# One queue for all cache loads, and a new order of the last tiles, in a batched attention decode step

## The chip, the cores and the metric

The kernel runs on one core of a Trainium2 chip. Its metric is the time of one execution on the device, in microseconds (us). Runs of this kernel lie within 2 us of each other, so a change of about 0.2% can be told from none.

The core has five engines that run side by side, each with its own instruction stream: TensorE (PE in the profile), VectorE (DVE), ScalarE (ACT), GpSimd (POOL) and SyncE (SP). Data comes from memory into the on-chip buffer by DMA. Sixteen DMA engines do the moving; a transfer is issued by an engine's instruction and goes through that engine's queue. SP's queue is q1 in the profile, ScalarE's is q10.

## What is computed

Two independent attention blocks, A and B, each with one new token for 8 sequences, 32 heads of size 128, and a cache of 4096 keys and values for each sequence and head:

```python
q = (x @ wq).reshape(B, Sq, H, Dh).transpose(0, 2, 1, 3)
scores = einsum("bhqd,bhkd->bhqk", q, k_cache) * (Dh ** -0.5)
p = softmax(scores, axis=-1)
o = einsum("bhqk,bhkd->bhqd", p, v_cache)
y = o.transpose(0, 2, 1, 3).reshape(B, Sq, H * Dh) @ wo
...
return concatenate([a, b], axis=-1)
```

Here B = 8, Sq = 1, D = 1024, H = 32, Sk = 4096, Dh = 128, all in bfloat16. The caches are 2 x 2 x 268 MB, and each element of them is used once.

## The kernel before, in words

**Tiles.** The work is cut into 128 units (NQ), each one sequence and four heads (HQ = 4). Unit n belongs to block `blk = n // 8` (four heads, all 8 sequences), and there are 16 blocks, 8 of A and then 8 of B. A unit has one K tile and one V tile of 4 MB, 128 partitions by 32 KB: 32 partitions to a head, and in each partition 128 consecutive cache rows of 128 numbers. A unit's K tile is worked in four chunks (NR = 4), so there are 512 steps (NS), and step s is chunk r of unit n with `n, r = divmod(s, 4)`.

**One step.** VectorE multiplies the chunk by the query in place (line 262), then adds the upper half of each row to the lower (L267, "fold"). TensorE adds up groups of 16 with an identity matrix (L275, "eacc"), and VectorE reduces what is left to 32 scores per partition (L281, "red"). After the fourth chunk VectorE takes the maximum (L287, L291), and ScalarE computes the exponentials, one instruction to a head (L297, L304), into the tile `PM`, a ring of two units.

**PV and after.** The products with V are 32 matmuls per unit on TensorE (L317, "PV"), in four parts, in a bank `pv_ps[n % 2]`. ScalarE copies the bank (L323), TensorE extracts the useful part of it (L331, "ext"). After the eighth unit of a block follow the sums of the exponentials (L338), the division (L345, L346) and the product with the block's rows of WO (L357, "proj"). After the last block of A and of B the result goes out (L362, L363, and two DMAs).

**Order.** There is no scheduler: the Python loop over `s` in the last part of `_build_kernel` adds each operation to its engine's list, and the engine runs its list in that order. An operation waits on semaphores for the operations that it depends on, and holds up what is behind it on the same engine. `make_pv` for unit v is called seven steps (PL = 7) after its first score step, two parts in step 4v + 7 and two in 4v + 8; ext, norm and proj follow 2, 3 and 4 steps after the first. The PVs so stand between the score matmuls of later units; the PVs of units 125 and 126 are called in steps 507 to 512, that of 127 in 515 and 516, after the last score step (511).

**Loads.** `order` is the sequence in which tiles take slots in a ring of five (NSLOT): K0, then K(n+1) and V(n) in turn. Tile i uses slot i % 5 and waits until tile i - 5 is done with: a K tile by its fourth eacc, a V tile by its last PV. `load_tiles`, called at the end of each step, issues the next tiles for which that operation has been put in the list. K tiles are issued from SP and V tiles from ScalarE. The last V tile is loaded in four pieces of 1 MB, each with its own semaphore. SP also issues x at the start, WQ (2 MB, 8 times, in packets of 2 KB) and WO (1 MB, 16 times, in packets of 2 KB), each when the one before it has been used.

Of the kernel before, what the change touches and what calls it, by code (L numbers as in the profile page):

```python
# [4 lines left out]
ACTF = mybir.ActivationFunctionType  # L5
ALU = mybir.AluOpType
AX = mybir.AxisListType
BF16 = mybir.dt.bfloat16
# [17 lines left out]
def _at(ops, key, none=None):  # L26

    first = key[0] if isinstance(key, tuple) else key
    return none if first < 0 else ops[key]


class _Program:
# [9 lines left out]
    def add(self, eng, emit, deps=(), dma_key=None):  # L42
        op = _Op(eng, emit, list(deps), dma_key)
        if dma_key is not None:
            self.counts[dma_key] = self.counts.get(dma_key, 0) + 16
            op.token = (dma_key, self.counts[dma_key])
        for d in op.deps:
            if not (d.eng == "pe" and eng == "pe"):
                d.sig = True
        self.ops[eng].append(op)  # L50
        return op
# [31 lines left out]
def _build_kernel(nc, caches, out):  # L83
    B, Sq, D = caches[0][0].shape
# [5 lines left out]
    HQ = 4  # L90
    MP = 128 // HQ
    T = Sk // MP
    CT = 32
    NR = T // CT
# [3 lines left out]
    NB = NC * H // HQ  # L98
    NQ = NB * B
    NS = NQ * NR  # L100
    NSLOT = 5
    PL = 7
# [3 lines left out]
    with es:  # L106
        block = es.enter_context(nc.Block())
        sb = lambda name, shape, dt: es.enter_context(nc.sbuf_tensor(name, shape, dt))
# [13 lines left out]
        s_sb = sb("s_sb", [128, 3, T], FP32)  # L122
        rmax = sb("rmax", [128, 2], FP32)
        ngm = sb("ngm", [128, 2], FP32)
        bias = sb("bias", [128, 2], FP32)
        rsum = sb("rsum", [128, 2, B], FP32)
        PM = sb("PM", [128, 2, T, HQ], BF16)
        accS = sb("accS", [128, 2, 512], BF16)
        rl = sb("rl", [128, 2, HQ * B], FP32)
        on_sb = sb("on_sb", [128, 2, HQ, B], BF16)  # L130
# [14 lines left out]
        P = _Program()  # L145
        add = P.add

        def dma(out_ap, in_ap, key, deps, eng="sp"):
            return add(eng, lambda e: e.dma_start(out_ap, in_ap), deps, dma_key=key)


        def pool_select(view, base, pattern, dep):
# [10 lines left out]
        for j in range(HQ):  # L163
            c_mask = add("dve", lambda e, j=j: e.memset(mask[MP * j:MP * (j + 1), j:j + 1], 1.0), [c_mask])
        c_PM = add("pool", lambda e: e.memset(PM[:], 0.0))
        c_pv = [add("dve", lambda e, t=t: e.memset(t[:], 0.0)) for t in pv_ps]

        opT, opMul, opEacc, opRed, opRmax, opNgm, opBias, opExp = {}, {}, {}, {}, {}, {}, {}, {}
        opPV, opAcc, opExt, opQb, opQbc, opQ, opQs, opWQ, opWO = {}, {}, {}, {}, {}, {}, {}, {}, {}
        opLsum, opNorm, opProj = {}, {}, {}  # L170
        last = {"misc": None}
        outs = []


        order = [("k", 0)]
        for n in range(NQ):
            if n + 1 < NQ:
                order.append(("k", n + 1))
            order.append(("v", n))
        pos = {kn: i for i, kn in enumerate(order)}  # L180
        issued = [0]

        def tile_of(kind, n):
            return ring[:, pos[(kind, n)] % NSLOT, :]

        def freed(i):

            kind, n = order[i]
            return opEacc.get(NR * n + NR - 1) if kind == "k" else opPV.get((n, NR - 1))

        def load_tiles():
            while issued[0] < len(order):
                i = issued[0]
                dep = None
                if i >= NSLOT:
                    dep = freed(i - NSLOT)
                    if dep is None:
                        return
                kind, n = order[i]
                blk, b = divmod(n, B)  # L200
                c, hb = divmod(blk, H // HQ)
                from_ = caches[c][1 if kind == "k" else 2][b, hb * HQ:(hb + 1) * HQ].rearrange("u (m t) d -> (u m) (t d)", m=MP)
                to = tile_of(kind, n)
                if i == len(order) - 1:
                    for r in range(NR):
                        cols = slice(r * CT * Dh, (r + 1) * CT * Dh)
                        opT[("v", n, r)] = dma(to[:, cols], from_[:, cols], ("vl", r), [dep], "act")
                else:
                    op = dma(to, from_, ("t", i % NSLOT), [dep], "act" if kind == "v" else "sp")
                    for r in range(NR):  # L210
                        opT[(kind, n, r)] = op
                issued[0] += 1
# [28 lines left out]
        def make_qbc(n):  # L241

            blk, b = divmod(n, B)

            def emit(e):
                for j in range(HQ):
                    i = e.matmul(misc[MP * j:MP * (j + 1), 0:Dh], selb[:, b, :], q_sb[:, blk % 4, j * Dh:(j + 1) * Dh],  # L247
                                 start=True, stop=True, tile_position=(0, MP * j))
                return i
            opQb[n] = add("pe", emit, [c_selb, opQs[blk], last["misc"]])  # L250
            opQbc[n] = last["misc"] = add(
                "act", lambda e: e.activation(qbc[:, n % 2, :], misc[:, 0:Dh], ACTF.Copy),  # L252
                [opQb[n], _at(opMul, NR * (n - 2) + NR - 1)])
# [41 lines left out]
        def make_exp(n):  # L295
            blk, b = divmod(n, B)
            opBias[n] = add("act", lambda e: e.activation(bias[:, n % 2:n % 2 + 1], ngm[:, n % 2:n % 2 + 1], ACTF.Copy, scale=scale),  # L297
                            [opNgm[n]] + _at(opExp, n - 2, []))
            opExp[n] = []
            for j in range(HQ):  # L300
                rows = slice(MP * j, MP * (j + 1))

                def emit(e, j=j, rows=rows):
                    return e.activation(PM[rows, n % 2, :, j], s_sb[rows, n % 3, :], ACTF.Exp, bias=bias[rows, n % 2:n % 2 + 1],  # L304
                                        scale=scale, accum_out=rsum[rows, blk % 2, b:b + 1])
                opExp[n].append(add("act", emit, [opBias[n], _at(opPV, (n - 2, NR - 1)), _at(opLsum, blk - 2), c_PM]))


        def make_pv(n, r):
            bank = pv_ps[n % 2]  # L310
            v = tile_of("v", n)

            def emit(e):
                for g in range(r * RG // NR, (r + 1) * RG // NR):
                    for q in range(4):
                        t = 4 * (4 * g + q)
                        i = e.matmul(bank[32 * q:32 * q + 4 * HQ, :], PM[:, n % 2, t:t + 4, :].rearrange("p t j -> p (t j)"),  # L317
                                     v[:, t * Dh:(t + 4) * Dh], start=(g == 0), stop=(g == RG - 1), tile_position=(0, 32 * q))
                return i
            opPV[(n, r)] = add("pe", emit, opExp[n] + [opT[("v", n, r)], _at(opAcc, n - 2), c_pv[n % 2]])  # L320
# [61 lines left out]
        make_q(0, 0)  # L382
        make_qbc(0)

        for s in range(NS + 16):
            n, r = divmod(s, NR)
            if s < NS:
                make_mul(s)
            if 1 <= s <= NS:
                make_red(s - 1)  # L390
            if r == 0 and 1 <= n <= NQ:
                make_rmax(n - 1)
            if s < NS:
                fold = make_fold(s)
            if r == 0 and 1 <= n <= NQ:
                make_ngm(n - 1)
                make_exp(n - 1)

            for k in range(2):
                v, w = divmod(s - PL - k, NR)  # L400
                if w == 0 and 0 <= v < NQ:
                    make_pv(v, 2 * k)
                    make_pv(v, 2 * k + 1)
                    if k == 1:
                        make_acc(v)
            v, w = divmod(s - PL - 2, NR)
            if w == 0 and 0 <= v < NQ:
                make_ext(v)
            if r == 2 and n + 1 < NQ:
                make_qbc(n + 1)  # L410
            if s < NS:
                make_eacc(s, fold)
            v, w = divmod(s - PL - 3, NR)
            if w == 0 and v >= 0 and v % B == B - 1 and v < NQ:
                make_norm(v // B)
            v, w = divmod(s - PL - 4, NR)
            if w == 0 and v >= 0 and v % B == B - 1 and v < NQ:
                make_proj(v // B)
            v, w = divmod(s - PL - 8, NR)
            if w == 0 and v >= 0 and v % B == B - 1 and v // B + 1 < NB:  # L420
                load_wo(v // B + 1)
            m, w = divmod(s, 2 * B * NR)
            if m == 0 and w == 3:
                make_q(0, 1)
            if w == 7 and m + 1 < NM:
                load_wq(m + 1)
            if w in (27, 35) and m + 1 < NM:
                make_q(m + 1, 0 if w == 27 else 1)
            load_tiles()
        assert issued[0] == len(order) and len(opProj) == NB  # L430

# [59 lines left out]
```

## Time and profile before

| | |
|---|---|
| Median of three runs | 2620.51 us (2619.95 to 2621.73) |
| Span of the profiled execution | 2618.7 us |
| The same execution's time | 2620.51 us |
| VectorE busy | 2080.5 us, 79% |
| TensorE matmuls busy | 1312.7 us, 50% |
| ScalarE busy | 445.8 us, 17% |
| Data moved | 1108.58 MB, 423 GB/s over the span |
| Share of q1 and q10 in the DMA engines' time | 51.1% and 47.9% |
| VectorE waiting for a K tile ahead of L262 | 501.0 us, 60 times |
| ScalarE waiting for the maximum ahead of L297 | 1594.5 us |

The page cuts the span into 40 slices of 65.5 us. In the row DMA each digit is the busy share of the DMA engines in tenths, and GB/s is what they moved. A row of a group of instructions has the line, the engine, the operation, what it writes and reads with its shape, how often, then busy time in us and mean ns of one, and then the idle time of the engine just before them with what ended most of it. A row of DMA issues has the tile and its source, the issuing queue, how many, the size of each and the median time from issue to landing in us. A row of a stretch of time has its bounds, its length, the busy us of PE, PEld (the weight loads of TensorE), DVE, ACT and POOL with the number of instructions, the share of full clock that TensorE was granted, the DMA share and GB/s.

### The profile page before, as it was taken

What the parts mean: (1) busy time and instruction counts of PE and PEld (TensorE: products, weight loads), DVE (VectorE), ACT (ScalarE), POOL (GpSimd) and SP (SyncE); (2) the same over time, 40 slices, a digit from 0 to 9 for tenths busy, and PEclk for the clock granted to TensorE, in tenths of its full rate; (3) what the DMA queues carried; (4) which work ended last, traced back from release to release, by engine and by line L of the source; (5) the groups of instructions that cost most, each with busy time, mean ns of one, the idle gap of its engine ahead of it and who ended that gap; (6) DMA issues with size and microseconds to landing.
All of it is one profiled execution on the core that took longest, in us unless ns stands there. A gap on an engine that the chain in (4) does not pass through costs nothing.

```text
span 2618.7 us, 18877 instructions
## 1 busy us (share of the span) xinstructions
PE 1312.7 (50%) x7568; PEld 368.8 (14%) x7568; DVE 2080.5 (79%) x1833; ACT 445.8 (17%) x1427; POOL 3.2 (0%) x15
## 2 busy tenths in 40 slices
PE   2555453653536535365353554536445364453645
PEld 0111110111101111011110111101111011111111
DVE  4988795986969869698695977959779696886957
ACT  0211111221112111121121211212112111111212
POOL 0000000000000000000000000000000000000000
PEclk9666665666667667676675766756766666666766
DMA  9999999999999999999999999999999999999996
GB/s 414 426 432 429 430 431 420 432 429 427 429 427 431 428 425 429 420 431 426 429 431 427 431 430 422 430 426 431 430 422 425 431 430 428 420 432 419 432 430 261
DMA packets 54247, 1108.58 MB, mean 423 GB/s; under 512 B 4576, under 2 KB 4608, under 8 KB 21008
## 3 DMA queue, kind: packets, MB, share of 16 engines
q1 hardware_dynamic: 35296, 570.50, 51.1%
q10 hardware_dynamic: 18864, 536.88, 47.9%
q8 instruction: 59, 0.97, 0.1%
q14 instruction: 28, 0.23, 0.0%
HBM read 1107.33 MB, written 0.03 MB: 423 GB/s over the span
## 4 chain that ended last, share of the span: by engine, by line
DVE 48%; DMA 32%; another core or an unknown queue 14%; PE 4%; issue 2%; ACT 1%; SPq 0%
DVE ring L262 27%; DMA ring<-in_A_k_cache_dram 15%; DVE ring L267 14%; DMA ring<-in_B_k_cache_dram 9%; DVE s_sb L281 6%; DMA ring<-in_B_v_cache_dram 5%; DMA ring<-in_A_v_cache_dram 3%; PE red L275 2%; PE pv L317 1%; DVE rmax L287 1%; PE proj L357 0%; ACT PM L304 0%; DVE ngm L291 0%; PE o L338 0%
## 5 line engine op out<-in xcount | busy, mean ns | idle before, releaser
L262 DVE TENSOR_TENSOR ring<-ring,qbc 128x4096 bf16<-128x4096 bf16 x512 | 1165.4, 2276 | 501.0 <-DMA ring<-in_A_k_cache_dram 259.4
L275 PE MATMUL red<-ring,ident 128*128 128x512 bf16 x2048 | 820.9, 545 | 938.8 <-DVE ring L267 938.8
L267 DVE TENSOR_TENSOR ring<-ring 128x2048 bf16<-128x2048 bf16 x512 | 622.1, 1215 | 0.0
L317 PE MATMUL pv<-ring,PM 128*16 128x512 bf16 x4096 | 397.2, 505 | 63.6 <-DMA ring<-in_B_v_cache_dram 36.6
L275 PEld LDWEIGHTS red<-ring,ident 128*128 128x128 bf16 x2048 | 203.7, 121 | 1378.9 <-DVE ring L267 1124.0
L281 DVE TENSOR_REDUCE s_sb<-red 128x32 f32<-128x512 f32 x512 | 350.0, 684 | 12.4 <-PE red L275 12.4
L304 ACT ACTIVATE PM<-s_sb,bias 32x128 bf16<-32x128 f32 x512 | 295.0, 576 | 15.1
L297 ACT ACTIVATE bias<-ngm 128x1 f32<-128x1 f32 x128 | 26.0, 203 | 1594.8 <-DVE ngm L291 1594.5
L331 PE MATMUL o<-E,accS 128*128 128x4 bf16 x512 | 33.6, 170 | 271.4 <-ACT accS L323 271.4
L317 PEld LDWEIGHTS pv<-ring,PM 128*16 128x16 bf16 x4096 | 98.9, 101 | 343.0 <-issue 215.7
L304 ACT ACTIVATION_READ_ACCUMULATOR PM<-s_sb,bias 32x1 f32 x512 | 128.1, 250 | 0.0
L252 ACT ACTIVATE qbc<-misc 128x128 bf16<-128x128 f32 x128 | 35.6, 278 | 370.6 <-PE misc L247 370.6
L323 ACT ACTIVATE accS<-pv 128x512 bf16<-128x512 f32 x128 | 76.4, 597 | 5.7 <-PE pv L317 2.2
L331 PEld LDWEIGHTS o<-E,accS 128*128 128x128 bf16 x512 | 22.8, 104 | 349.6 <-ACT accS L323 349.6
L233 PE MATMUL misc<-WQ,xT 128*8 128x512 bf16 x128 | 35.7, 429 | 20.7 <-DMA WQ<-in_A_wq_dram 20.7
L287 DVE TENSOR_REDUCE rmax<-s_sb 128x1 f32<-128x128 f32 x128 | 36.6, 286 | 4.4
L238 ACT ACTIVATE q_sb<-misc 8x512 bf16<-8x512 f32 x16 | 9.4, 587 | 171.7 <-PE misc L233 171.7
L247 PE MATMUL misc<-q_sb,selb 8*32 8x128 bf16 x512 | 37.1, 281 | 0.8 <-ACT q_sb L238 0.8
L247 PEld LDWEIGHTS misc<-q_sb,selb 8*32 8x32 bf16 x512 | 13.4, 96 | 104.3 <-issue 104.3
L291 DVE TRANSPOSE_TENSOR_REDUCE ngm<-rmax 128x1 f32<-128x32 f32 x128 | 26.2, 205 | 0.0
L338 PE MATMUL o<-rsum,mask 128*128 128x8 f32 x128 | 24.6, 320 | 0.0
L338 PEld LDWEIGHTS o<-rsum,mask 128*128 128x128 f32 x128 | 23.4, 274 | 0.0
(25 smaller groups left out, 55.7 us busy)
## 6 DMA issues: line engine op xcount, KB each, us to landing
ring<-in_A_v_cache_dram ACTq DMA_DIRECT2D x64, 4096.0 KB, 27.0
ring<-in_A_k_cache_dram SPq DMA_DIRECT2D x64, 4096.0 KB, 36.0
ring<-in_B_k_cache_dram SPq DMA_DIRECT2D x64, 4096.0 KB, 34.6
ring<-in_B_v_cache_dram ACTq DMA_DIRECT2D x63, 4096.0 KB, 26.0
WQ<-in_A_wq_dram SPq DMA_DIRECT2D x4, 2048.0 KB, 46.4
WO<-in_A_wo_dram SPq DMA_DIRECT2D x8, 1024.0 KB, 54.3
WQ<-in_B_wq_dram SPq DMA_DIRECT2D x4, 2048.0 KB, 63.5
WO<-in_B_wo_dram SPq DMA_DIRECT2D x8, 1024.0 KB, 54.9
```

The source lines that it names most:

```text
L233: i = e.matmul(misc[0:B, :], xT[:, (c * DC + k) * B:(c * DC + k + 1) * B], WQ[:, k, f * HQ * Dh:(f + 1) * HQ * Dh], start=(k == 0), stop=( ...
L247: i = e.matmul(misc[MP * j:MP * (j + 1), 0:Dh], selb[:, b, :], q_sb[:, blk % 4, j * Dh:(j + 1) * Dh], start=True, stop=True, tile_position ...
L262: opMul[s] = add("dve", lambda e: e.tensor_tensor(v, v, qbc[:, n % 2, :].unsqueeze(1).to_broadcast([128, CT, Dh]), ALU.mult), [opT[("k", n ...
L267: return add("dve", lambda e: e.tensor_tensor(v[:, :, 0:64], v[:, :, 0:64], v[:, :, 64:128], ALU.add), [opMul[s]])
L275: i = e.matmul(dst, ident[:], v[:, :, j, :], start=(j == 0), stop=(j == 3))
L281: opRed[s] = add("dve", lambda e: e.tensor_reduce(s_sb[:, n % 3, r * CT:(r + 1) * CT], red_ps[s % 2][:, :].rearrange("p (t w) -> p t w", w ...
L287: opRmax[n] = add("dve", lambda e: e.tensor_reduce(rmax[:, n % 2:n % 2 + 1], s_sb[:, n % 3, :], AX.X, ALU.max), [opRed[NR * n + NR - 1]])
L304: return e.activation(PM[rows, n % 2, :, j], s_sb[rows, n % 3, :], ACTF.Exp, bias=bias[rows, n % 2:n % 2 + 1], scale=scale, accum_out=rsum ...
L317: i = e.matmul(bank[32 * q:32 * q + 4 * HQ, :], PM[:, n % 2, t:t + 4, :].rearrange("p t j -> p (t j)"), v[:, t * Dh:(t + 4) * Dh], start=( ...
L323: opAcc[n] = add("act", lambda e: e.activation(accS[:, n % 2, :], pv_ps[n % 2][:], ACTF.Copy), [opPV[(n, NR - 1)], _at(opExt, n - 2)])
L331: x = e.matmul(o_ps[blk % 2][:, HQ * b:HQ * (b + 1)], accS[:, n % 2, i * 128:(i + 1) * 128], E16[:, i, :], start=(i == 0), stop=(i == 3))
L338: x = e.matmul(o_ps[blk % 2][:, 64 + B * j:64 + B * (j + 1)], mask[:, j:j + 1].to_broadcast([128, 128]), rsum[:, blk % 2, :], start=True, ...
```

## The change

All tile loads are issued from SP. The last five tiles come in the order K126, K127, V125, V126, V127, where it was K126, V125, K127, V126, V127. The PVs of the last three units start in steps 512, 514 and 516, after the last score step, so the exponentials of three units have to be kept, and `PM` becomes a ring of three. The order of all other operations is as before.

```diff
-        PM = sb("PM", [128, 2, T, HQ], BF16)
+        PM = sb("PM", [128, 3, T, HQ], BF16)
...
-        def dma(out_ap, in_ap, key, deps, eng="sp"):
-            return add(eng, lambda e: e.dma_start(out_ap, in_ap), deps, dma_key=key)
+        def dma(out_ap, in_ap, key, deps):
+            return add("sp", lambda e: e.dma_start(out_ap, in_ap), deps, dma_key=key)
...
         order = [("k", 0)]
-        for n in range(NQ):
-            if n + 1 < NQ:
-                order.append(("k", n + 1))
-            order.append(("v", n))
+        for n in range(NQ - 3):
+            order += [("k", n + 1), ("v", n)]
+        order += [("k", NQ - 2), ("k", NQ - 1), ("v", NQ - 3), ("v", NQ - 2), ("v", NQ - 1)]
...
-                        opT[("v", n, r)] = dma(to[:, cols], from_[:, cols], ("vl", r), [dep], "act")
+                        opT[("v", n, r)] = dma(to[:, cols], from_[:, cols], ("vl", r), [dep])
                 else:
-                    op = dma(to, from_, ("t", i % NSLOT), [dep], "act" if kind == "v" else "sp")
+                    op = dma(to, from_, ("t", i % NSLOT), [dep])
...
-                    return e.activation(PM[rows, n % 2, :, j], s_sb[rows, n % 3, :], ACTF.Exp, bias=bias[rows, n % 2:n % 2 + 1],
+                    return e.activation(PM[rows, n % 3, :, j], s_sb[rows, n % 3, :], ACTF.Exp, bias=bias[rows, n % 2:n % 2 + 1],
                                         scale=scale, accum_out=rsum[rows, blk % 2, b:b + 1])
-                opExp[n].append(add("act", emit, [opBias[n], _at(opPV, (n - 2, NR - 1)), _at(opLsum, blk - 2), c_PM]))
+                opExp[n].append(add("act", emit, [opBias[n], _at(opPV, (n - 3, NR - 1)), _at(opLsum, blk - 2), c_PM]))
...
+        pv_at = {max(NR * v + PL, NS + 2 * (v - NQ + 3) if v >= NQ - 3 else 0): v for v in range(NQ)}
...
             for k in range(2):
-                v, w = divmod(s - PL - k, NR)
-                if w == 0 and 0 <= v < NQ:
+                v = pv_at.get(s - k)
+                if v is not None:
                     make_pv(v, 2 * k)
                     make_pv(v, 2 * k + 1)
                     if k == 1:
                         make_acc(v)
-            v, w = divmod(s - PL - 2, NR)
-            if w == 0 and 0 <= v < NQ:
+            v = pv_at.get(s - 2)
+            if v is not None:
                 make_ext(v)
```

The calls of `make_norm`, `make_proj` and `load_wo` are put in terms of `pv_at` in the same way, 3, 4 and 8 steps after the PV's first. PV's matmuls read `PM[:, n % 3, ...]`.

More of the change, by code (lines that the diff above doesn't have):

```diff
@@ L316, in emit @@
                         t = 4 * (4 * g + q)
-                        i = e.matmul(bank[32 * q:32 * q + 4 * HQ, :], PM[:, n % 2, t:t + 4, :].rearrange("p t j -> p (t j)"),
+                        i = e.matmul(bank[32 * q:32 * q + 4 * HQ, :], PM[:, n % 3, t:t + 4, :].rearrange("p t j -> p (t j)"),
                                      v[:, t * Dh:(t + 4) * Dh], start=(g == 0), stop=(g == RG - 1), tile_position=(0, 32 * q))
@@ L412, in _build_kernel @@
                 make_eacc(s, fold)
-            v, w = divmod(s - PL - 3, NR)
-            if w == 0 and v >= 0 and v % B == B - 1 and v < NQ:
+            v = pv_at.get(s - 3)
+            if v is not None and v % B == B - 1:
                 make_norm(v // B)
-            v, w = divmod(s - PL - 4, NR)
-            if w == 0 and v >= 0 and v % B == B - 1 and v < NQ:
+            v = pv_at.get(s - 4)
+            if v is not None and v % B == B - 1:
                 make_proj(v // B)
-            v, w = divmod(s - PL - 8, NR)
-            if w == 0 and v >= 0 and v % B == B - 1 and v // B + 1 < NB:
+            v = pv_at.get(s - 8)
+            if v is not None and v % B == B - 1 and v // B + 1 < NB:
                 load_wo(v // B + 1)
```

## The prediction

> **What bounds the kernel now.** I read the page's load rows first, then the issues with their landing times, then the DMA queues over short stretches, the stretches that follow each stall, and last the end of the timeline.
>
> ```profile
> DMA  9999999999999999999999999999999999999996
> GB/s 414 426 432 429 430 431 420 432 429 427 429 427 431 428 425 429 420 431 426 429 431 427 431 430 422 430 426 431 430 422 425 431 430 428 420 432 419 432 430 261
> L262 DVE TENSOR_TENSOR ring<-ring,qbc 128x4096 bf16<-128x4096 bf16 x512 | 1165.4, 2276 | 501.0 <-DMA ring<-in_A_k_cache_dram 259.4
> ring<-in_A_v_cache_dram ACTq DMA_DIRECT2D x64, 4096.0 KB, 27.0
> ring<-in_A_k_cache_dram SPq DMA_DIRECT2D x64, 4096.0 KB, 36.0
> WO<-in_A_wo_dram SPq DMA_DIRECT2D x8, 1024.0 KB, 54.3
> ```
>
> All 16 DMA engines are busy from start to end at about 430 GB/s, and VectorE, the busiest engine (79%), stands 501.0 us waiting for K tiles. The loads are the bound. The odd row is the last: a 1 MB weight load takes 54.3 us to land, a 4 MB V tile 27.0. The DMA view of 2360 to 2376 us, with such a WO load on the way, says why (queue: packets, MB, share of the engines):
>
> ```profile
> q10 hardware_dynamic: 196, 5.37, 78.2%
> q1 hardware_dynamic: 475, 1.47, 23.0%
> ```
>
> q1 is SP's queue, q10 ScalarE's. SP sends many 2 KB packets and ScalarE few of 32 KB, so K and WO get a quarter of the time. The K tile behind WO comes late, VectorE stands still (21.79 us before the K at 2555.07), no slot comes free, and some 40 us later both queues are nearly empty. Of ten 20 us stretches in which that happens, these are five, with a quiet stretch of 140 us for comparison; the last two columns are DMA share and GB/s:
>
> ```profile
> 120.00:260.00 140.00, 79.66 (x440) 22.38 (x432) 116.68 (x102) 24.89 (x79) 0.00 (x0) 0.64 1.00 431
> 940.00:960.00 20.00, 9.97 (x56) 2.60 (x56) 19.93 (x19) 3.40 (x11) 0.00 (x0) 0.60 0.97 406
> 1600.00:1620.00 20.00, 12.64 (x76) 3.34 (x76) 19.97 (x18) 3.39 (x11) 0.00 (x0) 0.67 0.94 396
> 1920.00:1940.00 20.00, 11.50 (x64) 3.11 (x64) 19.96 (x18) 3.67 (x12) 0.00 (x0) 0.67 0.97 405
> 2240.00:2260.00 20.00, 11.01 (x60) 2.92 (x60) 19.96 (x19) 6.02 (x21) 0.00 (x0) 0.67 0.92 385
> 2400.00:2420.00 20.00, 11.94 (x66) 3.18 (x65) 19.96 (x18) 6.21 (x20) 0.00 (x0) 0.67 0.96 401
> ```
>
> The other five (from 440, 620, 1100, 1280 and 2560 us) have 421, 417, 403, 417 and 415 GB/s. The ten average 406.6, so against 431 they lose (431 - 406.6)/431 x 200 us = 11.3 us. The other K stalls cost VectorE time but no DMA time.
>
> Then the end:
>
> ```profile
> 2585.00:2590.00 5.00, 4.29 (x38) 1.01 (x36) 5.00 (x5) 0.00 (x0) 0.00 (x0) 0.76 1.02 429
> 2590.00:2595.00 5.00, 1.04 (x4) 0.31 (x4) 4.97 (x7) 2.98 (x10) 0.00 (x0) 0.92 0.81 339
> 2595.00:2600.00 5.00, 2.42 (x9) 0.75 (x10) 5.00 (x5) 0.13 (x1) 0.00 (x0) 0.50 0.00 0
> ```
>
> The data ends near 2594; the last piece of V lands at 2595.5 (issued at 2578.55, 17.0 to landing). The span ends at 2618.7: 23.2 us in which VectorE works off K126 and K127, since K125 had come late. The median of the runs is 2620.51, 1.8 more than the span, and I add that 1.8 at the end.
>
> **The change, part by part.**
>
> *V on SP's queue.* ScalarE loses 131 issues (64 + 63 + 4) at 0.334 us. It stands 1594.5 us waiting for ngm, which hides them: 0. SP gains 131 issues at 0.33 us, 43 us spread over waits of 2142.5 us for PV: 0. The waits themselves stay (a K slot comes free by the fourth score matmul, a V slot by the last PV), but now they stand in one line. K(n+1) lands at time 0; from the trace its slot is free at +17.3 (2555.07 to 2572.40) and V(n)'s at +18.3 (2573.37). A 4.19 MB tile at 431 GB/s takes 9.75 us, so in load order V(n) lands at 9.75, K(n+2) at 19.5, V(n+1) at 29.2 and K(n+3), issued at -1.2, at 39. The next issue, V(n+2), goes out at 17.3, when 39 - 17.3 = 21.7 us of data are still queued; that work hides every wait in the line. Without it each microsecond of lateness costs a microsecond. WO and WQ now pass in their turn: 1.05 MB at the 406 GB/s of 60 to 70 us, where WQ goes alone with K, is 2.6 us instead of 54.3. V(n) is needed by PV 14.2 us after K(n+1) (2569.25) and lands at 9.75; with a WO ahead at 12.4, with a WQ at 14.9. The last makes TensorE wait 0.7 us, in VectorE's slack of 19.5 - 16.2 = 3.3 us per tile pair (16.2 from 2555.07 to 2571.23): 0.
>
> What goes, then, is the running dry. Its bounds are 0 (the line stalls as often) and 20 (every byte at 431: 1108.58/431 ms = 2572, plus a first byte at 1.8, against 2594). The second can't be reached, since the 2 KB packets run at 406. I take the 11.3 that is seen in the ten stretches: **-11.3**.
>
> Here a rule of the Trainium skill speaks against the change. "DMA: Bandwidth & Descriptors", in Rules for kernel authors and in Issuing engines are not separate DMA queues, says that all issuing engines feed the same 16 DMA engines, and that spreading loads over them saves only issue time. Taken alone that makes this part worth nothing and the sum 11.3 us higher. The 78.2% against 23.0% above disagree for a stream with unequal packets: there the split decides which tile comes first.
>
> *The start.* The first large load was V0 from ScalarE at 0.74 us; now it is WQ at 1.49, behind x. The engines idle 0.75 us longer; at worst 1.5, if the slow first 20 us repeat, at best 0. I take **+0.8**. K0 lands near 20 us instead of 38, which helps only VectorE: 0.
>
> *The last five tiles.* K126, K127, V125, V126, V127. Let T be the landing of the last piece: 2595.5 - 11.3 + 0.8 = 2585.0. K126 lands four tiles before, T - 39.0. VectorE has finished K125 by then (it lands at T - 58.5, takes 16.2). From the first multiplication of K126 to the last exp the trace has 2571.23 to 2609.04 = 37.8 us, so exps(127) end at T - 1.2: the work that stood behind the stream is now beside it.
>
> *The last PVs.* PV125 and the first half of PV126 run after the last score matmul (2605.08 in the trace, 4.0 before the last exp, hence T - 5.2), 32 matmuls in 1.9 us, 16 in 0.95: done by T - 2.3. Then TensorE waits for the copy of bank 125, which stands behind exp(127) in ScalarE: 0.85 us from copy to next matmul (2609.06 to 2609.89 now), T - 0.35. Half of PV126 to T + 0.6; first half of PV127 to 1.55; extraction of 126 0.25; second half of PV127 to 2.75. From there the old tail: 2611.85 (last copy) to 2618.7 is 6.85, and 0.05 to get there. The span ends at T + 9.65, where it was T + 23.2. PV125 and PV126 are what is moved past the scores, 3.8 us: 2.85 of it lies beside the exps, the rest is in this sum.
>
> *Ring of 3 for the exps.* exp(127) waits for PV124 instead of PV125, without which the new order could not finish. The memset of PM grows from 0.95 to about 1.4 us on an idle GpSimd, needed near 36 us: 0.
>
> Sum: 2585.0 + 9.65 = 2594.65 of span, 2618.7 - 24.05. With 1.8 more: **2596.5 us**.
>
> **The rivals.** *The stream gains nothing.* One queue runs dry as often, and only the tail is shorter: 2595.5 + 0.8 + 9.65 + 1.8 = 2607.8. For it: the DMA share is at 9 throughout, and most stalls cost no DMA time. Against it: in 2360 to 2376 us K was held up beside V, and the dip at 2400 us followed. 14%.
>
> *The tail is not hidden.* The stream is shorter, but scores lag so far that 23.2 us still follow it: 2585.0 + 23.2 + 1.8 = 2610.0. For it: VectorE is 79% busy and runs without a gap over the last 50 us. Against it: it had idled 21.79 us just before, and K126 comes no earlier than 19.5 us after K125, against 16.2 of work. 10%.
>
> *SP stands blocked at a weight load (the slower case).* The issues themselves sometimes hold SP: the longest WO issue is 23.25 us, a K behind one 15.7. ScalarE's V went round that; now V waits too. Data of 21.7 us covers a block; a longer one drains the engines. There are 24 weight loads, so the whole gain of 24 us is lost once each drains the engines for 1.0 us, a block of 22.7 each. If all were as long as the longest, 23.25, each would leave 1.55 us dry, 37 us in all, and the time would be 2634. Against it: the median WO issue is 0.435 to 1.07 us, and the long ones fall where V takes most of the bandwidth and SP's own packets hardly move. 6%.
>
> **How the numbers follow.** Forecast 66%, rivals 14, 10 and 6%, something that cancels to within the bound 4%. The measurement can tell about 0.2%, 5.2 us. The forecast's own range is 2588 (most of the 20 us) to 2600 (three of the ten stretches stay). To leave no more than 2 in 10 out it must take in the first two rivals: 2588 to 2611. Faster 0.90, within 0.2% 0.04, slower 0.06.
>
> **What would show it.** Right: the ten dips gone and GB/s at 427 or more in nearly all slices, WO landing in tens of us only because tiles stand before it, q1 alone with the data, no K stall near 20 us, the last exp within 2 us of the last landing, and some 10 us after it. Wrong: a gap at each tile on the single queue (0.1 us at 256 tiles would eat the gain; the stretch 40 to 56 us, 99.4% on q1 at 428 GB/s, shows none), VectorE still behind when K126 lands, or SP issues of over 20 us with idle DMA engines after them.

## The result, and the profile after

The changed kernel takes 2603.76 us (median of six runs, 2603.38 to 2604.32); the kernel before, run on the same chips, 2622.43 (six runs, 2619.95 to 2628.06, so they spread more than the first three had). The ratio is 0.9927, with a 95% interval of 0.9914 to 0.994. The forecast was 2596.5, which is 7.3 us too low. The profiled execution took 2604.08 us with a span of 2602.3, so its span is 16.4 below that of before, where 24.05 had been forecast.

The load rows of the changed kernel's page:

```profile
GB/s 410 427 429 430 431 427 429 431 429 432 425 430 431 430 429 428 431 429 432 429 424 431 430 430 431 427 430 432 429 431 421 428 433 427 433 429 431 430 430 314
q1 hardware_dynamic: 54160, 1107.38, 99.5%
L262 DVE TENSOR_TENSOR ring<-ring,qbc 128x4096 bf16<-128x4096 bf16 x512 | 1165.9, 2277 | 476.0 <-DMA ring<-in_A_k_cache_dram 247.4
ring<-in_A_k_cache_dram SPq DMA_DIRECT2D x64, 4096.0 KB, 39.9
WO<-in_A_wo_dram SPq DMA_DIRECT2D x8, 1024.0 KB, 38.1
```

WO now lands a little sooner than a K tile issued beside it; before, it took twice as long as a V tile. The slices at 419 to 422 GB/s are gone but for one. The ten stretches that averaged 406.6 GB/s now have 428, 436, 428, 424, 428, 435, 432, 435, 432 and 416, on average 429.4. One queue carries all the data at the rate that two did.

VectorE's idle time has hardly changed (476.0 us for 501.0), but its waits for K have. These rows are from the view of waits (us in total, times, the longest), for B's cache: first before, then after.

```profile
DVE ring L262 <- DMA ring<-in_B_k_cache_dram: 241.5, 27, 26.5
```

```profile
DVE ring L262 <- DMA ring<-in_B_k_cache_dram: 228.6, 62, 8.6
```

For B, few long stalls have become many short ones: K comes once per unit, in its turn. Over both caches, and after the first tile, the longest wait is 9.7 us now, where it was 27.9.

At the end, however, the stream no longer stops sharply, as it had before. The stretches of the changed kernel:

```profile
2575.00:2580.00 5.00, 2.35 (x6) 0.43 (x4) 5.00 (x5) 1.25 (x6) 0.00 (x0) 0.50 0.97 406
2580.00:2585.00 5.00, 1.89 (x4) 0.43 (x4) 5.00 (x5) 0.00 (x0) 0.00 (x0) 0.50 0.68 282
2585.00:2590.00 5.00, 4.53 (x32) 1.41 (x36) 1.60 (x4) 1.25 (x5) 0.00 (x0) 0.50 0.36 149
2590.00:2595.00 5.00, 4.95 (x84) 1.89 (x72) 0.00 (x0) 2.48 (x8) 0.00 (x0) 0.88 0.03 11
```

From 2580 on the DMA share falls to 0.68, then 0.36, which suggests that some of the 16 DMA engines are done and others still work (the table below bears it out). The last piece of V is there when the slowest is, at 2592.05 by the trace's landing records (2595.5 before). The order of the end is as drawn up in the forecast, here in the timeline:

```profile
2590.76 0.58 ACT L304 ACTIVATE PM<-s_sb,bias 32x128 bf16<-32x128 f32 x1
...
2591.37 0.60 ACT L323 ACTIVATE accS<-pv 128x512 bf16<-128x512 f32 x1
...
2594.22 1.04 PE L317 MATMUL pv<-ring,PM 128*16 128x512 bf16 x16
...
2599.51 0.68 DVE L362 CAST orow<-proj 8x512 bf16<-8x512 f32 x1 [1.77 <-PE proj L357]
```

The last exp ends at 2591.34, 0.7 us before the last landing, the last PV at 2595.26, and the span 10.25 after the landing.

So two questions stood: which part brought the shorter tail, and why the end of the stream moved by only 3.5 us when the dips in the mean rate are gone.

### The profile page after: what moved, and what is told of

It reads as the page before. It is cut to its first block, busy times and chain, and to the rows that moved or that the text cites. A ratio compares the mean times of both kernels' runs of the same rounds, so it can differ in the third digit from the quotient of the medians.

```text
span 2602.3 us, 18878 instructions
## 1 busy us (share of the span) xinstructions
PE 1383.7 (53%) x7568; PEld 384.3 (15%) x7568; DVE 2086.1 (80%) x1833; ACT 445.7 (17%) x1427; POOL 3.6 (0%) x15
## 4 chain that ended last, share of the span: by engine, by line
DMA 70%; DVE 22%; PE 7%; ACT 1%; issue 1%; SPq 0%
DMA ring<-in_B_k_cache_dram 31%; DMA ring<-in_A_k_cache_dram 30%; DVE ring L262 12%; DVE ring L267 6%; DMA ring<-in_A_v_cache_dram 4%; DMA ring<-in_B_v_cache_dram 4%; PE red L275 3%; DVE s_sb L281 3%; PE pv L317 2%; ACT PM L304 1%; PE proj L357 1%; PE o L338 0%; PE misc L233 0%; DVE rmax L287 0%; ACT accS L323 0%
## 5 line engine op out<-in xcount | busy, mean ns | idle before, releaser
L262 DVE TENSOR_TENSOR ring<-ring,qbc 128x4096 bf16<-128x4096 bf16 x512 | 1165.9, 2277 | 476.0 <-DMA ring<-in_A_k_cache_dram 247.4
L275 PE MATMUL red<-ring,ident 128*128 128x512 bf16 x2048 | 887.2, 583 | 992.2 <-DVE ring L267 992.2
L275 PEld LDWEIGHTS red<-ring,ident 128*128 128x128 bf16 x2048 | 214.3, 127 | 1461.9 <-DVE ring L267 1204.1
```

The source lines that it names most:

```text
L262: opMul[s] = add("dve", lambda e: e.tensor_tensor(v, v, qbc[:, n % 2, :].unsqueeze(1).to_broadcast([128, CT, Dh]), ALU.mult), [opT[("k", n ...
L275: i = e.matmul(dst, ident[:], v[:, :, j, :], start=(j == 0), stop=(j == 3))
```

## The experiments

The trace holds 16 landings for each tile, as many as there are DMA engines, and I read them as one from each engine when its share has landed. For the last piece of V they are, sorted, as us after the first of them (each row is one trace):

```
                   last      after the first of the 16
before             2595.5    0.0 0.0 0.1 0.1 0.2 0.3 0.3 0.3 0.4 0.4 0.7 0.8 0.9 1.0 1.0 1.4
changed            2592.0    0.0 0.0 0.1 0.2 0.3 0.3 3.5 6.7 6.8 6.9 7.0 7.1 7.2 8.3 8.5 10.9
queue alone        2592.0    0.0 0.1 0.1 0.1 0.1 0.4 3.5 6.9 6.9 7.0 7.0 7.0 7.1 8.5 8.8 11.0
quarter of PV      2592.1    0.0 0.1 0.2 0.3 0.4 0.6 2.1 2.2 2.2 2.5 2.5 3.5 3.5 3.6 3.7 11.0
VectorE padded     2607.6    0.0 0.2 0.2 0.3 0.4 0.4 1.5 1.7 1.8 2.2 3.1 3.2 3.4 3.7 3.7 14.5
VectorE in pairs   2590.1    0.0 0.0 0.1 0.1 0.2 0.3 5.6 8.8 9.0 9.1 9.2 9.3 9.4 9.5 10.7 10.8
```

In the changed kernel this spread grows along the run: 2.2 us at 333, 4.1 at 676, 8.1 at 1343, 10.9 at 1990. Behind a held issue it falls to 7.9 at 2024, and it is back at 10.9 at 2482. In the kernel before it does not add up: half of the 255 tiles are under 2.9 us, 18 are over 5, up to 9.2, and each time it falls back.

**The queue alone.** The kernel before with V issued from SP.

```diff
-                        opT[("v", n, r)] = dma(to[:, cols], from_[:, cols], ("vl", r), [dep], "act")
+                        opT[("v", n, r)] = dma(to[:, cols], from_[:, cols], ("vl", r), [dep])
...
-                    op = dma(to, from_, ("t", i % NSLOT), [dep], "act" if kind == "v" else "sp")
+                    op = dma(to, from_, ("t", i % NSLOT), [dep])
```

> Only the queue of V changes; order of the last tiles, PVs and the ring of two stay as before. Theory (the queue brings nearly all of it: tiles come in load order, no K is held up by a weight load): the last landing is that of the changed kernel, near 2592 us, K127 lands 19.6 before it, the exps of 127 end 21.7 after that (2587.38 to 2609.04 in the trace of before), so 2 us after the last landing, and the old tail of 9.65 follows: span 2604, time about 2605.5. Rival (the shorter tail comes from the new order of the last tiles): the 23 us behind the last landing stay, span about 2615. Rival (the queue brings nothing): span 2618.7.

Measured: 2607.73 us, ratio 0.994 (0.9925 to 0.9955), span 2603.7, last landing 2592.0. The span of the trace meets the first theory to 0.3 us; the median is 2.2 over the 2605.5 expected, since the traced run is the fastest of the four. In that trace the queue by itself shortens the tail from 23.2 to 11.7 us: the multiplication of K125 starts at 2533.51 us after 5.85 of idling, instead of 2555.07 after 21.79, and the last exp ends 2 us behind the last landing.

**The order alone.** The changed kernel with V back on ScalarE's queue.

```diff
-            return add("sp", lambda e: e.dma_start(out_ap, in_ap), deps, dma_key=key)
+            return add(eng, lambda e: e.dma_start(out_ap, in_ap), deps, dma_key=key)
...
-                    op = dma(to, from_, ("t", i % NSLOT), [dep])
+                    op = dma(to, from_, ("t", i % NSLOT), [dep], "act" if kind == "v" else "sp")
```

> Only the order of the last five tiles, the late PVs and the ring of three; V stays on ScalarE's queue. Theory (the late K125 behind the last weight load sets the end of the scores, whatever the order after it): exps of 127 end at 2609 as before, and the changed kernel's 11.0 us from last exp to end follow: span 2620, time no better than before. Rival (the order hides the scores beside the last V tiles): span near 2606.

Measured: 2614.43 us, ratio 0.9968 (0.9955 to 0.9981), span 2613.4, last landing 2597.3, which is 1.8 later than before. Neither theory: the order alone is worth 5.3 us of span in the traces, 8.1 by the medians. K125 still comes late, but less so, in the timelines of the kernel before and of this one:

```profile
2555.07 2.29 DVE L262 TENSOR_TENSOR ring<-ring,qbc 128x4096 bf16<-128x4096 bf16 x1 [21.79 <-DMA ring<-in_B_k_cache_dram]
2548.57 2.29 DVE L262 TENSOR_TENSOR ring<-ring,qbc 128x4096 bf16<-128x4096 bf16 x1 [13.19 <-DMA ring<-in_B_k_cache_dram]
```

In the new order fewer V tiles are asked for beside the last K tiles, so these get more of the time: from 2536 to 2555 us ScalarE's queue moves nothing here, where it had 51.3% of the DMA time before. I had taken the lateness of K125 as given. The gains of the two parts, 15.0 and 5.3 us of span, are together more than the 16.4 of both; both make the same late K less late.

**Weights in wide packets.** The kernel before, with WQ and WO read in packets of 8 KB in place of 2 KB. The bytes are as many, but other elements of the weights are read, so the output is another.

```diff
-            opWQ[m] = dma(WQ[:], caches[c][3][:, col:col + HM * Dh].rearrange("(k p) n -> p k n", p=128),
+            opWQ[m] = dma(WQ[:].rearrange("p (k z) n -> p k (z n)", k=2), caches[c][3][256 * p:256 * p + 256, :].rearrange("(k p) n -> p k n", p=128),
...
-            opWO[blk] = dma(WO[:], caches[c][4][hb * HQ * Dh:(hb + 1) * HQ * Dh, :].rearrange("(h p) n -> p h n", p=128),
+            opWO[blk] = dma(WO[:].rearrange("p h n -> p (h n)"), caches[c][4][hb * HQ * Dh:(hb + 1) * HQ * Dh, :].rearrange("(p h) n -> p (h n)", p=128),
```

> The kernel before, but WQ and WO are read in packets of 8 KB in place of 2 KB (same bytes; other elements of the weights, so the output is another). Theory (two queues are served packet by packet, so a load of many small packets holds up the K behind it): WO lands in about 25 us in place of 54, no K stall over 10 us, the ten dips in GB/s gone or under half, K125 in time and so a tail of about 12 us; the last landing 2580 to 2590, span 2592 to 2602. Rival (the dips come from the two queues and five slots as such): dips and tail stay, span about 2610, lower only by the faster weight loads. If the DMA engines drift apart when they never run dry, the 16 landings of the last piece spread over more than 5 us, where before they spread over 1.4.

Measured: 2606.64 us, ratio 0.9939 (0.9922 to 0.9956), span 2604.6, last landing 2584.6 with a spread of 5.5. The dips and the last landing came as the theory had it; three other things did not. WO still lands in 50 to 53 us, because the time from issue holds the K tiles ahead of it (the last one is issued at 2469.75 and its first packet moves at 2500.7). VectorE still waits 14 to 25 us for the K tiles behind the weight loads, where no stall over 10 had been expected. The tail is 20.0 us instead of 12, so that the span is above the expected range. K125 in this kernel's timeline:

```profile
2539.49 2.29 DVE L262 TENSOR_TENSOR ring<-ring,qbc 128x4096 bf16<-128x4096 bf16 x1 [15.38 <-DMA ring<-in_B_k_cache_dram]
```

From K124's landing to K125's there are 38.0 us before, 31.6 here and 22.1 in the changed kernel, for the same 1 MB of WO between them. While WO is on its way, the DMA view has these rows, for 2500 to 2515 us of this kernel and for 2515 to 2530 of the kernel before:

```profile
q10 hardware_dynamic: 159, 4.62, 71.8%
q1 hardware_dynamic: 174, 1.78, 28.0%
```

```profile
q10 hardware_dynamic: 198, 5.96, 92.9%
q1 hardware_dynamic: 194, 0.38, 6.6%
```

Without packets of under 512 bytes these are 141 of V beside 125 of WO and 18 of K here, and 182 of V beside 187 of WO before. So the engines take packets from the two queues in turn, those of 32 KB like those of 2 KB. They take them one by one: the time from one packet of WO to another has its peak at 1.5 us here and 1.3 us before, which is one packet of each queue. Each DMA engine has 8 packets of WO here, each behind a 32 KB packet of V: 8 x (1.21 + 0.31) = 12.2 us by the trace's packet times, and with the 19.4 of two tiles 31.6. The same sum for the 32 packets of 2 KB before would be 32 x (1.21 + 0.09) + 19.4 = 61 us and not 38.0, because it holds only while V's queue has packets; there it ran out at about 2533 us, and the remaining 279 packets of WO passed in 4 us. The ten stretches are at 426.3 GB/s on average. And yet the dips bring little by themselves: of the 10.9 us by which the last landing is earlier, 8.8 are the packets' own price by their mean times (16400 of 87 ns against 4096 of 314, over 16 engines). That points the same way as the changed kernel: a dip in the mean rate need not be lost time at the end.

**Fewer instructions on TensorE.** The changed kernel with a quarter of the PV matmuls.

```diff
-                    for q in range(4):
+                    for q in range(1):
```

> The changed kernel with 8 of the 32 PV matmuls of each unit (three quarters of the PV product left out); all loads as they are. This takes away 6144 of 18878 instructions, 24 of the 59 packets of 16 KB in which instructions are fetched. Theory (these packets fall on some of the 16 DMA engines more than on others; the engines that carry them end last and set every landing): the spread of the 16 landings of the last piece falls from 10.9 to about 6.5 us, the last landing from 2592 to about 2587.6, the span to about 2596. Rival (some DMA engines are slower for another reason): spread 11 and last landing 2592 stay, the span falls by 2 us at most, for the shorter last PVs.

Measured: one run, 2603.39 us, span 2601.6, last landing 2592.1, spread 11.0. As for the end, the theory falls; but the table shows that it is half right. With the page's row

```profile
q8 instruction: 35, 0.57, 0.1%
```

for 59 before, the nine engines that were 3.5 to 8.5 us behind are 2.1 to 3.7 behind, and only the last stays where it was, at 11.0. So TensorE's instruction fetches do make DMA engines late, but the slowest one is late for another reason. The other fetch queue, q14, has 28 packets of 8 KB in the span of either kernel. Fifteen of the changed kernel's follow each other at 159 to 186 us, and a K tile that lands just after one of these is 1.0 us late. Three K tiles of the changed kernel in turn, and the DMA queue in 1606 to 1608 us:

```profile
1587.57 2.29 DVE L262 TENSOR_TENSOR ring<-ring,qbc 128x4096 bf16<-128x4096 bf16 x1 [3.19 <-DMA ring<-in_B_k_cache_dram]
1608.02 2.29 DVE L262 TENSOR_TENSOR ring<-ring,qbc 128x4096 bf16<-128x4096 bf16 x1 [4.20 <-DMA ring<-in_B_k_cache_dram]
1627.40 2.29 DVE L262 TENSOR_TENSOR ring<-ring,qbc 128x4096 bf16<-128x4096 bf16 x1 [3.15 <-DMA ring<-in_B_k_cache_dram]
```

```profile
q1 hardware_dynamic: 29, 0.92, 108.7%
q14 instruction: 1, 0.01, 1.0%
```

From 1587.57 to 1608.02 are 20.45 us, from there to 1627.40 19.38.

**More instructions on VectorE.** The changed kernel with writes that nobody reads.

```diff
+        pad = sb("pad", [128, 4], FP32)
...
                 fold = make_fold(s)
+                if s < NS - 12:
+                    for j in range(4):
+                        add("dve", lambda e, j=j: e.memset(pad[:, j:j + 1], 0.0))
```

> The changed kernel with 16 writes of one unused column on VectorE per unit, none in the last three units; loads and results unchanged. VectorE has 3.3 us of slack per unit, the writes take about 1.6. Theory (the slowest DMA engine is the one that also fetches VectorE's instructions, 8 KB on q14 every 165 us, and each such fetch puts every later landing 1.0 us back): with some 16 instructions more to 15.6 per unit the fetches double, the spread of the 16 landings of the last piece goes from 10.9 to 20 to 25 us, the last landing from 2592 to 2602 to 2606, the span to 2612 to 2616. Rival (that engine is slow for a reason of its own): spread 11, last landing 2592, span 2602.

Measured: one run, 2618.96 us, span 2617.2, last landing 2607.6. The pages of the changed kernel and of this one have

```profile
q14 instruction: 29, 0.23, 0.0%
```

```profile
q14 instruction: 44, 0.36, 0.0%
```

One of the 29 is a packet of under 512 bytes. So there are 16 fetches of 8 KB more, and the last landing is 15.6 us later. The series that came at 159 to 186 us comes at 79 to 95 here. Work of some 2,000 tiny instructions on an engine with time to spare has cost 15.2 of the 18.7 us that the change had brought. The spread is 14.5 and not 20 or more, since the other engines ran dry: at 1360 and 2000 us, where SP is held up at a weight load, the rate falls to 326 and 324 GB/s over 20 us.

Those two holds, or a VectorE that frees its slots later, could be thought to be the cause instead. Tile by tile, the landings of this kernel against those of the changed one rule both out (us later; first column: when the tile lands in the changed kernel; last: how many more 8 KB packets q14 has had by then):

```
          last of the 16    middle    first    packets more
 342.5         2.1           -0.4      0.3          2
 666.1         4.1            0.2      0.2          4
1352.2         8.1            0.4      1.6          8
1377.1         9.0            4.0      8.1          9
1999.6        11.9            4.2      8.1         12
2024.4        11.8            8.4     11.8         12
2562.7        15.6            6.9     11.9         16
```

The last of the 16 falls back by about 1.0 us with each packet, while the middle stays within 0.4 us up to 1352: not the whole stream is late, but one engine. Each hold (1352 to 1377, 2000 to 2024) sets back the engines that are ahead by 6.5 and 3.7 us, and the last one by no more than its fetches.

**Fewer instructions on VectorE.** Multiply and fold over two chunks at once, in all but the last three units.

```diff
+            w = width(s)
+            if w == 0:
+                opMul[s] = opMul[s - 1]
+                return
+            v = tile_of("k", n)[:, r * CT * Dh:(r + w) * CT * Dh].rearrange("p (t d) -> p t d", d=Dh)
...
+        def width(s):
+            return 1 if s >= NS - 12 else 2 - 2 * (s % 2)
```

> The changed kernel with multiply and fold over two chunks at once (10 VectorE instructions per unit in place of 14), in the last three units as before. Theory (fetches): a quarter of VectorE's fetches go, the slowest engine loses 3 us and the next ones, with TensorE's fetches, take its place 2.5 us earlier: last landing 2589.6, spread 8 to 9, span about 2600. Rival: last landing and span unchanged.

Measured: 2601.60 us, ratio 0.9922 (0.9907 to 0.9936), span 2600.7, last landing 2590.1, 24 fetches on q14. The last landing comes 2.0 us sooner, and the slowest engine now ends with the next ones, presumably those that fetch for TensorE (the last two at 10.7 and 10.8). The spread is not 8 to 9, because the fastest engines end earlier too.

**The order K, K, K, and both together.** One more K tile ahead of the last V tiles, with and without the pairs.

```diff
-        for n in range(NQ - 3):
+        for n in range(NQ - 4):
             order += [("k", n + 1), ("v", n)]
-        order += [("k", NQ - 2), ("k", NQ - 1), ("v", NQ - 3), ("v", NQ - 2), ("v", NQ - 1)]
+        order += [("k", NQ - 3), ("k", NQ - 2), ("k", NQ - 1)] + [("v", n) for n in range(NQ - 4, NQ)]
...
-        pv_at = {max(NR * v + PL, NS + 2 * (v - NQ + 3) if v >= NQ - 3 else 0): v for v in range(NQ)}
+        pv_at = {max(NR * v + PL, NS + 2 * (v - NQ + 3) if v >= NQ - 4 else 0): v for v in range(NQ)}
```

> The changed kernel with K125, K126, K127 ahead of V124 to V127, and PV124 in step 510. Theory (the end now hangs on the scores, which end 0.7 us before the last landing, and on the PVs behind them): exps end some 4.5 us before the last landing, PV of the last piece alone follows it, and the span ends 7.4 us after it in place of 10.3: 2599.5. Rival (PVs and the copies between them, not the scores, hold the end): 10 us after the last landing as now, 2602.

> Both of the two: pairs on VectorE and the K, K, K order. If both theories hold, last landing 2589.6 and span 2597, time about 2599. If only the order does, span 2599.5; if only the fetches, 2600.

Measured: the order alone 2602.30 us, span 2600.3, last landing 2592.0; both 2599.66, ratio 0.9914 (0.9897 to 0.9931), span 2597.7, last landing 2589.9. The tail after the landing is 8.3 and 7.8 us; TensorE now waits for the data, as the timeline of the first of them has it:

```profile
2592.08 0.61 PE L317 MATMUL pv<-ring,PM 128*16 128x512 bf16 x8 [1.40 <-DMA ring<-in_B_v_cache_dram]
```

It is 0.4 to 0.9 us more than worked out, but the bound at the end is the stream again.

These were measured on another chip than the changed kernel, so that one and "both" were run side by side.

> The changed kernel as it is, on the same chip as the next run, so that the two can be compared: about 2603.8, 0.993 of before.

> Pairs on VectorE and the K, K, K order once more, beside the changed kernel on one chip. Theory: 4 to 4.6 us less than the changed kernel (span 2597.7 against 2602.3 in the single traces), 0.9915 of before. Rival (the difference was between chips): the same as the changed kernel within 1 us.

Measured: 2603.53 (2603.36 to 2603.93) and 2600.47 us (2599.49 to 2601.24), ratios to before 0.9922 (0.9908 to 0.9935) and 0.991 (0.9896 to 0.9923). The runs of the two don't overlap. Both together beat the changed kernel by 3.1 us, less than the 4 to 4.6 expected.

## Why the prediction was right or wrong

**The bound and the mechanism were right.** The loads set the time; with two queues a WO load of small packets holds up the K behind it, and on one queue it passes in its turn. The packet counts and the sum for the wide packets (31.6 us) show this. The page "DMA: Bandwidth & Descriptors" of the Trainium skill, in Queues, rings and completion order, says that a DMA engine takes packets from its queues in turn; the counts (141 beside 125, 182 beside 187) agree. The rule cited in the forecast, that spreading loads over issuing engines brings no bandwidth, also held: one queue moves 426 GB/s over the span, two moved 423. What mattered was which tile comes first.

**The step that failed: "I take the 11.3 that is seen in the ten stretches".** It should have been 4.3. With the start's +0.8, the forecast moved the last landing by -10.5 us, and it moved by -3.5. Of the 7.7 us by which the span fell less than forecast, 7.0 are this step and 0.6 the tail. The 11.3 is the loss of rate averaged over 16 DMA engines. The last landing belongs to one of them, the one with most to do. Before, the landings say, the engines that were ahead ran dry in the dips and waited; that levelled the 16 (a spread of 1.4 us at the end) and cost the slowest little. The holds of the padded kernel show the same thing directly: the mean rate falls to 324 GB/s, the first engines lose 3.7 us and the last none. In the changed kernel hardly any engine waits, the mean rate is full, and the engines drift apart until the ones ahead are done early, from 2580 on. The average was right and belonged to the wrong engine.

**The start was right.** The first 20 us run at 369 GB/s in place of 387, which is (387 - 369)/431 x 20 = 0.8 us, and K0 lands at 19.2.

**The tail had the right size and the wrong origin.** It went from 23.2 to 10.25 us after the landing, 9.65 had been worked out. Within it, the exps end 0.7 us before the landing (1.2 expected) and PV127 3.2 after it (2.75). But the forecast put it to the order of the last five tiles. The queue alone makes it 11.7. The order on top of it is worth 1.4 us of span in the two traces and 4.0 by the medians; the two kernels were not run side by side, so its size stays open between these.

**The range and the rivals.** The forecast's own range, 2588 to 2600, does not hold the measured 2603.76; the stated one does because it was widened for the first two rivals. That is prudence and some luck, not the sum. "The stream gains nothing" gave 2607.8, 4.0 us from the measured time, and so was nearer in number than the forecast with its 7.3: the stream gained a third of what was forecast. Its reason was wrong, since the dips did go. "SP stands blocked" exists as a mechanism: eight issues of the changed kernel are held for 8 to 16 us. At 1989.38 us it is a V tile's, for 15.63 us behind a WQ load, and 2000 to 2005 us run at 359 GB/s, 0.8 us on average. It hits the engines that are ahead (the spread falls from 10.9 to 7.9 us there), and nothing shows that it moved the end. "The tail is not hidden" did not come.

## What to carry to other kernels

Where a stream is the bound, its end is set by the slowest of the 16 DMA engines. A loss of mean bandwidth can then be more than there is to gain (11.3 against 4.3 us here), and the 16 landings of each transfer, tile by tile, tell how much of it is real. Loads that are needed in a known order belong on one queue when their packets differ much in size. When one engine of a kernel bound by DMA has time to spare, its number of instructions can still count, because their fetches ride on the same DMA engines (16 fetches more cost 15.6 us here).

## What the runs showed of the hardware that was not expected

Instruction fetches go through the DMA engines, between the data packets. Taking 6144 instructions off TensorE took 24 packets of 16 KB from q8 and brought eight of the sorted landings 3.5 to 4.8 us forward; 2,000 more on VectorE added 16 packets of 8 KB on q14 and put the last landing 15.6 us back, about 1.0 each. In the packet records of the trace an 8 KB fetch takes 0.33 us, and the data packet after it 1.87 in place of 1.22; the two make up the 1.0. The fetches that grow with VectorE's instructions add up on the engine that ends last, which fits a fixed engine for them; the trace does not number the DMA engines, so that it is always the same one is inferred from the steps, not seen. The same page of the skill lists, in the same section, "refill" among the runtime's uses of queue row 14. If the profile's q14 is that row, its instruction packets agree; TensorE's fetches are on q8 here.
